# First scale group loaded as two blocks on the ScalarE queue, c moved to the SP queue, statistics of three x tiles moved between engines, engine orders redone

## The chip, the cores and the metric

The kernel runs on one core of one Trainium2 chip. The metric is the device time of one execution in microseconds (us); where several executions are given, the number is their median. Most executions of a kernel agree within a few tenths of a per cent; some runs are called slow (over 1.5% above the fastest of the same kernel) and are left out of ratios. A profile is one execution, and its times count from the start of the span, which is 1.8 to 1.9 us shorter than the device time. Profiles of two kernels therefore show where time lies; the medians and ratios say how much it is.

## The reference, cut to what matters

A diffusion block: c gives modulation vectors, x is normalised, scaled and shifted, then attention and a gated residual follow. B, N, D are 2, 256, 1152, all in bfloat16.

```python
mod = (_silu(c) @ w_mod).reshape(B, 6, 1, D)
shift_a, scale_a, gate_a, shift_m, scale_m, gate_m = [mod[:, i] for i in range(6)]
h = _layernorm(x, axis=-1) * (1 + scale_a) + shift_a
qkv = h @ wqkv
# ... q, k, v cut from qkv
p = _softmax(jnp.einsum('bqd,bkd->bqk', q, k) * D ** (-0.5), axis=-1)
a = jnp.einsum('bqk,bkd->bqd', p, v) @ wo
return x + gate_a * a
```

## The kernel before: the parts that matter

x stands in four tiles of 128 rows (288 KB each). The key projection comes first: the normalised tiles are transposed by TensorE (PE), multiplied by 1 + scale (`s1p`, from `psS`) into `hTs`, and multiplied by the rows of wK (nine loads of 288 KB, one per k). The scale vector is itself a product, of silu(c) and `w_scale`. `w_scale` is loaded in four groups of 128-column blocks; group 0 holds blocks 0 and 1 (576 KB). The first wK steps (k = 0 and 1) need group 0.

```python
nc.scalar.preload_act_table_set("natural_log_exp_and_others")
load_x(syn, 0)                                   # syn: the queue issued by SP
sca.dma_start(out=c_sb, in_=c.rearrange(...))    # sca: the queue issued by ScalarE
# ...
def scale_mods(gi, lo, hi):                      # psS[:, j] += w_scale block j times silu(c)
    k0, k1 = S_GROUPS[gi]                        # ((0, 2), (2, 4), (4, 6), (6, 9))
    for kk in range(lo, hi):
        for j in range(k0, k1):
            ten.matmul(psS[:, j, :], lhsT=wS[gi][:, kk, ...], rhs=sc_rhs(kk), ...)
# ...
junk(2)                      # filler matmuls on a tile of ones, their results are thrown away
ten.transpose(cT_ps, c_sb, ident[...])
# ... three activations make silu(c)
junk(10)
# ... SP's loads, in order: x1, x2, group 0, wK0, wK1, x3, group 1, wK2, group 2, ...
transposes(0, 0)
scale_mods(0, 0, 9)
transposes(0, 1)
k_step(0, 0, P)              # first step with wK
```

Every engine works through its own list in the order in which the program pins it. The scheduler gives each load one of a small set of semaphores, and a load that reuses one waits until the load that used it before has landed.

## Time and profile before

| | kernel before |
|---|---|
| device time, median of the first three runs | 98.47 us (98.41 to 98.59) |
| span of the profile | 95.7 us |
| PE busy | 91.0 us, 95% |
| first matmul on x | 7.69 us |
| scale group 0: issued, landed, used | 2.11, 7.64, 7.91 us |
| scale group 1: landed, used | 11.32, 11.52 us |

First the page. The first lines give the span and the engines' busy time; the rows below cut the span into 40 slices and give tenths of a slice busy. PEclk is the share of the full TensorE clock that was granted. PEld is the load of weights into PE; DVE is VectorE, ACT ScalarE, POOL GpSimd.

```profile
span 95.7 us, 1886 instructions
PE 91.0 (95%) x771; PEld 60.9 (64%) x771; DVE 64.1 (67%) x131; ACT 32.3 (34%) x75; POOL 15.7 (16%) x11
PE   3899999999999999999999999999999999999980
PEclk9999999999999999999999999999999999999999
DMA  1999999999999999999993001122000000303122
```

PE is the limit from end to end, and the loads run flat out for the first half. What counts is when PE's useful work starts and whether it is ever idle after that. The timeline of PE says it (start, duration, engine, operation, output and inputs, shapes; `xN` merges N instructions):

```profile
2.90 0.19 PE L70 MATMUL cT_ps<-ident,c_sb 18*128 18x18 bf16 x1 [0.42 <-DMA c_sb<-in_c_dram]
3.45 4.45 PE L70 MATMUL acc_t<-ones_w 128*128 128x512 bf16 x10
7.69 0.42 PE L70 MATMUL tp_t<-ident,xn 128*128 128x128 bf16 x2
7.91 0.69 PE L70 MATMUL psS<-scT_rep,wS_all 128*128 128x56 bf16 x18
8.44 0.55 PE L70 MATMUL tp_t<-ident,xn 128*128 128x128 bf16 x7
8.98 0.66 PE L70 MATMUL acc_t<-hTs,wK 128*128 128x128 bf16 x9
...
11.52 0.63 PE L70 MATMUL psS<-scT_rep,wS_all 128*128 128x56 bf16 x18
```

Ten fillers end at 7.90, 0.6 us after the first normalised tile is there (7.31); group 0's 18 small matmuls start 0.27 us after its load has landed, and apart from the wait for c in the first line none of these lines shows a wait. The issues of DMA between 2.0 and 2.4 us, with size and time from issue to landing, give the load of group 0 (issued at 2.11, so landed at 7.64) and the one ahead of it, x tile 2, which landed at 5.60:

```profile
wS_all<-in_w_scale_dram SPq DMA_DIRECT2D x1, 576.0 KB, 5.5
x_sb<-in_x_dram SPq DMA_DIRECT2D x1, 288.0 KB, 4.0
```

Last, stretches of 4 us with each engine's busy time, and PEclk third from the end and GB/s last:

```profile
8.00:12.00 4.00, 4.00 (x91) 3.86 (x89) 3.02 (x11) 3.23 (x6) 0.00 (x0) 1.00 1.04 408
12.00:16.00 4.00, 3.93 (x64) 3.55 (x61) 3.56 (x14) 3.26 (x11) 0.00 (x0) 1.00 1.03 402
16.00:20.00 4.00, 4.00 (x60) 3.66 (x58) 1.25 (x9) 1.61 (x5) 0.00 (x0) 1.00 1.04 401
```

PE is busy for nearly all of each stretch at the full clock, while about 400 GB/s come in.

### The profile page before, as it was taken

Reading aid. Unit: us, or ns where it says so; the run is one execution under the profiler, and the core shown is the slowest. Engines: PE = TensorE matmul, PEld = TensorE weight load, DVE = VectorE, ACT = ScalarE, POOL = GpSimd, SP = SyncE. Lnnn points to the kernel's source line nnn. Section 1 sums busy time; section 2 is a strip of 40 time slices with the busy share of each in tenths; the row PEclk is TensorE's granted clock in tenths of the full one; section 3 lists DMA queues with packets and bytes.
Section 4 is the critical chain, followed back from the end, with each engine's and each line's share of the span. In section 5 each row is a group of like instructions: output and inputs, shape, how many; then the busy total and the mean of one; then the engine's idle time right before and its main releaser. Section 6 shows DMA issues by size and latency. Waiting matters only on the chain.

```text
span 95.7 us, 1886 instructions
## 1 busy us (share of the span) xinstructions
PE 91.0 (95%) x771; PEld 60.9 (64%) x771; DVE 64.1 (67%) x131; ACT 32.3 (34%) x75; POOL 15.7 (16%) x11
## 2 busy tenths in 40 slices
PE   3899999999999999999999999999999999999980
PEld 0237989988899644444458765565568766556570
DVE  2487887050552999999999939910009599998780
ACT  5496988020421900003950084342335400000010
POOL 3020000000000000000000000079999900010000
PEclk9999999999999999999999999999999999999999
DMA  1999999999999999999993001122000000303122
GB/s 23 366 337 414 402 397 398 400 420 403 416 416 419 414 413 419 422 422 416 419 400 159 0 0 55 45 65 54 8 0 0 0 0 0 123 7 123 75 100 72
DMA packets 7379, 21.59 MB, mean 225 GB/s; under 512 B 2123, under 2 KB 2891, under 8 KB 7371
## 3 DMA queue, kind: packets, MB, share of 16 engines
q1 hardware_dynamic: 7200, 21.42, 57.7%
q8 instruction: 6, 0.10, 0.4%
q10 hardware_dynamic: 171, 0.05, 0.2%
q14 instruction: 2, 0.02, 0.0%
HBM read 19.76 MB, written 1.44 MB: 221 GB/s over the span
## 4 chain that ended last, share of the span: by engine, by line
PE 93%; DMA 2%; DVE 0%; ACT 0%; issue 0%
PE ps L70 67%; PE acc_t L70 19%; PE psS L70 3%; DMA c_sb<-in_c_dram 2%; PE psH L70 2%; PE tp_t L70 2%; ACT o_sb L70 0%; DVE hTs L70 0%; PE cT_ps L70 0%; DVE s1p L70 0%; ACT L104 0%
## 5 line engine op out<-in xcount | busy, mean ns | idle before, releaser
L70 POOL PARTITION_ALL_REDUCE gate_bc<-gacc x2 | 13.7, 6887 | 56.8 <-DVE gacc L70 56.8
L70 DVE SCALAR_TENSOR_TENSOR gacc<-wg_all,scT_f,gacc 128x1152 f32<-128x1152 bf16 x16 | 22.4, 1416 | 0.4
L70 PE MATMUL ps<-wV,hT 128*128 128x384 bf16 x108 | 17.7, 326 | 0.0
L70 PE MATMUL ps<-hT,wQ 128*128 128x512 bf16 x81 | 17.7, 379 | 0.0
L70 PEld LDWEIGHTS <-wK 128*128 128x128 bf16 x180 | 16.1, 98 | 1.8 <-issue 0.2
L70 PE MATMUL ps<-rows_t,attnT 128*128 128x384 bf16 (+3 forms) x108 | 17.0, 319 | 0.0
L70 PEld LDWEIGHTS <-attnT 128*128 128x128 bf16 x117 | 11.2, 98 | 6.4
L70 PEld LDWEIGHTS <-hT 128*128 128x128 bf16 x108 | 10.6, 98 | 6.9
L70 PE MATMUL acc_t<-hTs,wK 128*128 128x256 bf16 (+1 forms) x144 | 14.8, 259 | 0.1
L70 PEld LDWEIGHTS <-wQ 128*128 128x128 bf16 x81 | 7.9, 98 | 9.4
L70 ACT CAST v_sb<-ps 128x384 bf16<-128x384 f32 x12 | 5.8, 481 | 13.9 <-PE ps L70 13.9
L70 DVE CAST attnT<-ps 128x512 bf16<-128x512 f32 (+1 forms) x6 | 3.5, 603 | 9.5 <-PE ps L70 9.5
L70 ACT CAST qkT<-ps 128x512 bf16<-128x512 f32 x11 | 5.6, 610 | 12.6 <-PE ps L70 12.6
L70 DVE TENSOR_TENSOR ga<-ps,gate_bc 128x384 f32<-128x384 f32 (+3 forms) x12 | 6.4, 537 | 1.1 <-PE ps L70 1.0
L70 PE MATMUL acc_t<-ones_w 128*128 128x512 bf16 x12 | 5.5, 630 | 1.4 <-DVE ones_w L70 1.4
L70 DVE TENSOR_TENSOR o_sb<-ga,x_sb 128x384 bf16<-128x384 f32 (+3 forms) x12 | 6.5, 542 | 0.4
L70 ACT CAST o_sb<-ps 128x192 bf16<-128x192 f32 x1 | 0.3, 319 | 17.3 <-PE ps L70 17.3
L70 DVE CAST qkT<-acc_t 128x512 bf16<-128x512 f32 (+1 forms) x5 | 2.5, 576 | 4.5 <-PE acc_t L70 4.5
L70 DVE BATCH_NORM_STATS2 st_t<-x_sb 128x6 f32<-128x384 bf16 x6 | 3.1, 550 | 2.5 <-DMA x_sb<-in_x_dram 2.5
L70 PE MATMUL ps<-hTs,wK 128*128 128x256 bf16 x36 | 4.3, 272 | 0.0
L70 ACT ACTIVATE hTs<-xnT,s1p 128x128 bf16<-128x128 bf16 (+1 forms) x9 | 3.3, 417 | 2.8 <-DVE s1p L70 2.3
L70 PEld LDWEIGHTS <-ones_w 128*128 128x128 bf16 (+1 forms) x13 | 1.6, 135 | 4.1 <-issue 2.6
(59 smaller groups left out, 76.4 us busy)
## 6 DMA issues: line engine op xcount, KB each, us to landing
wK<-in_wk_dram SPq DMA_DIRECT2D x9, 288.0 KB, 8.3
rows_t<-in_w_shift_dram SPq DMA_DIRECT2D x3, 864.0 KB, 11.7
wQ<-in_wq_dram SPq DMA_DIRECT2D x3, 864.0 KB, 14.3
wg_all<-in_w_gate_dram SPq DMA_DIRECT2D x3, 864.0 KB, 14.4
wV<-in_wv_dram SPq DMA_DIRECT2D x3, 864.0 KB, 17.1
rows_t<-in_wo_dram SPq DMA_DIRECT2D x3, 864.0 KB, 17.1
wS_all<-in_w_scale_dram SPq DMA_DIRECT2D x3, 576.0 KB, 6.4
x_sb<-in_x_dram SPq DMA_DIRECT2D x4, 288.0 KB, 3.6
```

Source lines behind the costliest of these rows:

```text
L70: r = fn(*a, **k)
```

## The change

The intent, as far as the diff tells it: load the two blocks of group 0 from a second queue, so that they come in beside x tile 2 and PE can begin with block 0 alone, one filler earlier; take the statistics of tile 3 off ScalarE (it does tile 2 instead of tiles 1 and 3); redo all engine orders for that. Also c moves from the ScalarE queue to second place on SP.

```diff
+    load_x(syn, 0)
+    syn.dma_start(out=c_sb, in_=c.rearrange("b (k p) -> (b k) p", p=P))
     nc.scalar.preload_act_table_set("natural_log_exp_and_others")
-    load_x(syn, 0)
-    sca.dma_start(out=c_sb, in_=c.rearrange("b (k p) -> (b k) p", p=P))
...
+    def load_block(j):
+        cols = slice(KT * P * j, KT * P * (j + 1))
+        sca.dma_start(out=wS_all[:, cols], in_=w_scale[...])
...
     sca.activation(out=e_sb, in_=cT_ps, func=ACT.Exp, scale=-1.0)
+    load_block(0)
     sca.activation(out=e_sb, in_=e_sb, func=ACT.Ln, bias=1.0)
     sca.activation(out=e_sb, in_=e_sb, func=ACT.Exp, scale=-1.0)
+    load_block(1)
...
-    junk(10)
+    junk(9)
... (the orders; on SP now x2, x1, wK0, wK1, x3, group 1, ...; on PE:)
+    block_mods(0)
+    block_mods(1)
     transposes(0, 0)
+    transposes(0, 1)
... (statistics: tile 1 from ScalarE to VectorE, tile 2 from VectorE to ScalarE,
     tile 3 from ScalarE to VectorE)
```

More of the change, by code (lines that the diff above doesn't have):

```diff
@@ L123 @@
     wS_all = wmpool.tile([P, KT * D], BF16, tag="wS")
-    S_GROUPS = SCALE_GROUPS
+    S_GROUPS = ((0, 2), (2, 4), (4, 6), (6, 9))
     wS = []
@@ L133, in load_scale @@
         syn.dma_start(out=wS_all[:, cols], in_=src)
+    def load_block(j):
+        cols = slice(KT * P * j, KT * P * (j + 1))
+        sca.dma_start(out=wS_all[:, cols], in_=w_scale[P * cols.start : P * cols.stop].rearrange("(p n) -> p n", p=P))
     def load_wK(k):
@@ L277, in scale_mods, with block_mods @@
                 )
+    def block_mods(j):
+        w_j = wS_all[:, KT * P * j : KT * P * (j + 1)].rearrange("p (kk n) -> p kk n", kk=KT)
+        for kk in range(KT):
+            ten.matmul(
+                psS[:, j, :], lhsT=w_j[:, kk, :], rhs=sc_rhs(kk),
+                start=False, stop=(kk == KT - 1), skip_group_check=True,
+            )
     def copy_s1p(gi):
@@ L305, in k_step_b1 @@
             )
-    junk(10)
+    junk(9)
+    load_x(syn, 2)
+    stat_chunk(0, 0)
+    stat_sum(2)
     stat_chunk(0, 1)
-    stat_chunk(0, 0)
     load_x(syn, 1)
-    stat_sum(1)
-    load_x(syn, 2)
     stat_chunk(0, 2)
+    silu_c()
+    block_mods(0)
     stat_aggr(0)
-    silu_c()
-    stat_chunk(2, 2)
-    stat_chunk(2, 1)
     stat_ln(0)
     stat_exp(0)
+    stat_chunk(1, 1)
+    stat_chunk(1, 2)
+    stat_chunk(1, 0)
     norm(0, 0, 2)
+    stat_aggr(1)
+    stat_sq(2)
+    block_mods(1)
     transposes(0, 0)
-    load_scale(0)
-    scale_mods(0, 0, 9)
     norm(0, 2, KT)
-    stat_chunk(2, 0)
-    stat_aggr(2)
+    transposes(0, 1)
     scaled_tp(0, 0, vec)
     scaled_tp(0, 1, vec)
-    stat_sq(1)
-    stat_ln2(1)
+    stat_ln(1)
+    copy_s1p(0)
+    load_wK(0)
     stat_exp(1)
-    copy_s1p(0)
     norm(1, 0, 2)
-    load_wK(0)
-    transposes(0, 1)
-    load_wK(1)
-    norm(1, 2, KT)
-    stat_ln(2)
     k_step(0, 0, P)
     transposes(1, 0)
+    load_wK(1)
+    k_step(1, 0, P)
+    stat_ln2(2)
+    norm(1, 2, KT)
+    stat_exp(2)
+    evac_tp(0, 1, sca, 0, 7)
+    transposes(1, 1)
+    norm(2, 0, 2)
+    evac_tp(1, 1, sca, 0, 7)
+    scaled_tp(1, 1, vec)
     scaled_tp(1, 0, vec)
-    evac_tp(0, 1, sca, 0, 7)
-    k_step(1, 0, P)
     load_x(syn, 3)
-    transposes(1, 1)
+    stat_chunk(3, 2)
+    stat_chunk(3, 0)
+    stat_chunk(3, 1)
+    norm(2, 2, KT)
     k_step(0, P, N)
-    scaled_tp(1, 1, vec)
     k_step(1, P, N)
-    stat_exp(2)
-    norm(2, 0, 2)
-    evac_tp(1, 1, vec, 0, 7)
-    norm(2, 2, KT)
     load_scale(1)
@@ L355 @@
     copy_s1p(1)
-    scaled(2, 0, vec)
     transposes(2, 0)
     transposes(2, 1)
-    evac_tp(2, 1, vec, 0, 7)
-    stat_sum(3)
-    stat_sq(3)
-    stat_ln2(3)
+    stat_aggr(3)
+    stat_ln(3)
     stat_exp(3)
-    norm(3, 0, 2)
+    evac_tp(2, 1, sca, 0, 7)
+    scaled(2, 0, vec)
+    evac_tp(2, 0, vec, 0, 2)
+    scaled_t(0, 2, vec)
     load_wK(2)
     k_step(2, 0, N)
-    norm(3, 2, KT)
-    evac_tp(2, 0, sca, 0, 2)
-    scaled_t(0, 2, vec)
-    transposes(3, 0)
-    load_scale(2)
-    scaled_t(3, 2, vec)
-    scaled(3, 0, sca)
-    evac_tp(3, 0, sca, 0, 2)
-    scaled_t(0, 3, sca)
+    norm(3, 0, 2)
+    scaled(3, 0, sca)
+    load_scale(2)
+    transposes(3, 0)
+    evac_tp(3, 0, sca, 0, 2)
+    norm(3, 2, KT)
     scale_mods(2, 0, 9)
+    transposes(3, 1)
     copy_s1p(2)
+    scaled_t(0, 3, vec)
+    evac_tp(3, 1, vec, 0, 7)
     scaled_t(5, 2, vec)
-    scaled_t(2, 2, sca)
-    transposes(3, 1)
     load_wK(3)
     k_step(3, 0, N)
-    evac_tp(3, 1, vec, 0, 7)
+    scaled_t(1, 2, sca)
+    scaled_t(3, 3, vec)
+    scaled_t(1, 3, sca)
+    scaled_t(3, 2, sca)
     alloc_b1()
     k_step_b1(0, [1, 2, 3, 4])
-    scaled_t(1, 2, vec)
-    scaled_t(3, 3, vec)
-    load_wK(5)
-    scaled(5, 0, vec)
+    scaled(4, 0, sca)
+    scaled_t(5, 3, sca)
+    k_step_b1(3, [1, 2, 3, 4])
     k_step_b1(0, [0])
-    scaled_t(5, 3, sca)
-    k_step(5, 0, N)
-    k_step_b1(3, [1, 2, 3, 4])
-    scaled_t(1, 3, vec)
-    scaled_t(4, 2, sca)
-    scaled_t(2, 3, sca)
+    scaled_t(4, 2, vec)
+    k_step_b1(1, [1, 2, 3, 4])
+    scaled_t(2, 3, vec)
+    k_step_b1(1, [0])
+    load_scale(3)
+    scaled(5, 0, sca)
+    scaled_t(2, 2, vec)
     k_step_b1(2, [1, 2, 3, 4])
-    load_scale(3)
-    k_step_b1(5, [0])
     scale_mods(3, 0, 9)
-    scaled_t(4, 3, vec)
-    scaled(4, 0, sca)
+    scaled_t(4, 3, sca)
     copy_s1p(3)
-    scaled(6, 0, vec)
-    scaled_t(6, 2, vec)
+    scaled(6, 0, sca)
+    scaled_t(6, 2, sca)
     scaled_t(6, 3, vec)
     scaled(7, 0, vec)
-    scaled_t(7, 2, vec)
-    scaled_t(7, 3, vec)
-    scaled(8, 0, vec)
+    scaled_t(7, 2, sca)
+    scaled_t(7, 3, sca)
+    scaled(8, 0, sca)
     scaled_t(8, 2, sca)
-    scaled_t(8, 3, sca)
+    scaled_t(8, 3, vec)
     load_wK(4)
+    load_wK(5)
     load_wK(6)
@@ L417 @@
     load_rest()
-    k_step_b1(1, [0])
-    k_step_b1(1, [1, 2, 3, 4])
     k_step_b1(2, [0])
@@ L424 @@
     k_step_b1(4, [1, 2, 3, 4])
+    k_step(5, 0, N)
+    k_step_b1(5, [0])
     k_step_b1(5, [1, 2, 3, 4])
@@ L669 @@
         pin(rec.seq)
-SCALE_GROUPS = ((0, 2), (2, 4), (4, 6), (6, 9))
+SCALE_BLOCKS = ((0, 1), (1, 2), (2, 4), (4, 6), (6, 9))
 _OUTS = [((2, 256, 1152), 'bfloat16')]
@@ L690, in _packed @@
     scale = rows(w_mod[:, D : 2 * D]).transpose(1, 0, 2)
-    scale = _np.concatenate([scale[:, :, k0 * P : k1 * P].reshape(-1) for k0, k1 in SCALE_GROUPS])
+    scale = _np.concatenate([scale[:, :, k0 * P : k1 * P].reshape(-1) for k0, k1 in SCALE_BLOCKS])
     return {
```

## The prediction

> **What bounds the kernel now.** TensorE. On the page PE is busy 91.0 of 95.7 us; the chain of waits is 93% PE, and from 3.52 us on it has one gap (12.16 to 12.72). Three stages by timeline: filler matmuls until the first data (useful work starts at 7.69; filler starts 0.43 us apart); from 7.7 to 20 us PE rides just behind the loads; then pure matmul to 93 us. The Trainium skill, "TensorE: Matmul & The Clock Gate", Part 1, says cold matmuls run at half rate; the trace agrees (0.43 us per 512 columns before 8.0 us, 0.109 per 256 after). Loads stream at one 288 KB unit per 0.74 us: x0 lands at 3.60, the third unit 5.60, scale group 0 7.64, wK0 8.39, group 1 11.32 (used 11.47), group 3 17.55 (used 18.05). So PE has 0.2 to 0.5 us to gain at most.
>
> **What the change does.**
> 1. One filler of 0.43 us goes.
> 2. c goes behind x0 on one queue. Now it lands at 2.85 alone on its own; behind x0 (last packets start 3.05, landing 3.60) I expect 3.65. The transpose of c and all filler after it start 0.75 later; with one filler less, PE's useful start moves from 7.69 to about 8.05, later.
> 3. The two blocks. Block 0 is issued after the first e_sb activation (4.1), starts about 1.0 us later, shares engines half and half with wK0 and wK1: lands about 7.15. Block 1 reuses the semaphore of x tile 1, which lands third (5.6), so ScalarE stops there until 5.6; it lands about 8.65, against 7.64 for the whole group. The skill, "DMA: Bandwidth & Descriptors", "Issuing engines are not separate DMA queues", says queues interleave on the same engines; bytes are equal, so nothing is gained.
> 4. ScalarE: that stop plus the two issues (0.5 each) and the sum of tile 2 (1.16) come before rstd of tile 0: 7.7 instead of 6.05; norm of tile 0 7.7 instead of 6.56, upper part 8.2 instead of 6.80. First wK step 9.6 instead of 8.98. Its evacuation of tile 0 (0.9) ends about 10.9 and holds the transposes of tile 1.
> 5. VectorE: tile 3 statistics (3 x 0.46 paced) stand at about 11.2 to 12.6, in front of norm of tile 2 and the second s1p copy. The second scale group's matmuls start at 12.3 (11.68 now), the 256-wide step of wK2 at 13.7 (12.72 now).
> 6. Saved: ScalarE's 2.4 us pass over tile 3; not on PE's chain now.
>
> **On the critical path.** Replaying the new order with durations of this trace: PE late by 0.35 at its start, 0.6 at the first wK step, 0.95 at wK2, about 0.8 at wK3 (15.6 instead of 14.83). After that the delay is carried unchanged. 98.47 + 0.8 = 99.3 us.
>
> **Predicted: 99.3 us, range 98.4 to 100.2.** Chances: faster by over 2% 0.01; within 2% 0.94; slower by over 2% 0.05.
>
> **What would show it.** c landing near 3.65 and PE idle from 2.5 to it; first block matmul at 8.05 to 8.2 and a short PE wait before block 1; ScalarE idle before its second issue until x tile 1 lands; first rstd after 7.4; statistics of tile 3 just ahead of the second s1p copy; PE gaps totalling about 1 us between 8 and 14, none after 16.
>
> **What would make it wrong.** c landing before x0, or block 1 by 8.0: then near 98.3. Filler ending before the clock rises, or a gap that delays the rise: useful work at half rate, 1 us or more worse. ScalarE issues far shorter than 0.5 us: 0.3 us better.

## The result

| | before | after |
|---|---|---|
| device time, median of 4 runs each | 98.44 us (98.36 to 98.59) | 105.57 us (105.13 to 106.24) |
| ratio of the fast runs | 1 | 1.0728 (95% interval 1.0661 to 1.0796) |
| span of the profile | 95.7 us | 104.1 us |
| first filler after c, c's transpose | 3.45, 2.90 us | 4.15, 3.59 us |
| first scale matmul | 7.91 us | 11.99 us |
| first wK matmul | 8.98 us | 15.38 us |
| matmuls of scale group 1 start | 11.52 us | 19.69 us |

A ratio is the mean time of one kernel's fast runs over the mean of the other's fast runs of the same rounds, so it is not quite the ratio of the medians. The change makes the kernel 7% slower.

The page after:

```profile
span 104.1 us, 1884 instructions
PE 93.0 (89%) x768; PEld 62.9 (60%) x770; DVE 63.5 (61%) x129; ACT 32.6 (31%) x77; POOL 15.6 (15%) x11
PE   3691169999999999999999999999999999999990
PEclk9999855899999999999999999999999999999999
DMA  3899999999999999999910000112200000203042
```

Two things are new, both in the first eight slices: a hole in the PE row, and a dip of PEclk right behind it. DMA has no hole, so the loads were not missing; others came first. The same two pieces stand in the timeline of PE:

```profile
3.59 0.19 PE L70 MATMUL cT_ps<-ident,c_sb 18*128 18x18 bf16 x1 [1.11 <-DMA c_sb<-in_c_dram]
4.15 4.02 PE L70 MATMUL acc_t<-ones_w 128*128 128x512 bf16 x9
11.99 0.41 PE L70 MATMUL psS<-scT_rep,wS_all 128*128 128x56 bf16 x9 [3.82 <-DMA wS_all<-in_w_scale_dram]
14.03 0.60 PE L70 MATMUL psS<-scT_rep,wS_all 128*128 128x56 bf16 x9 [1.64 <-DMA wS_all<-in_w_scale_dram]
...
15.38 1.17 PE L70 MATMUL acc_t<-hTs,wK 128*128 128x128 bf16 x9
...
19.69 0.63 PE L70 MATMUL psS<-scT_rep,wS_all 128*128 128x56 bf16 x18
```

The fillers end at 8.17, then PE waits 3.82 us for block 0 and 1.64 us for block 1. The nine wK matmuls take 1.17 us, which took 0.66 us before. The stretches of 4 us show why:

```profile
8.00:12.00 4.00, 0.18 (x2) 0.02 (x2) 1.84 (x6) 3.54 (x10) 0.00 (x0) 1.00 1.02 400
12.00:16.00 4.00, 2.36 (x33) 2.25 (x34) 1.12 (x5) 0.37 (x1) 0.00 (x0) 0.54 1.04 415
16.00:20.00 4.00, 4.00 (x54) 4.00 (x52) 2.65 (x8) 1.44 (x2) 0.00 (x0) 0.61 1.04 393
```

PE was idle almost throughout 8 to 12 us; from 12.31 to 19.14 us the clock record is at one half. In that time the useful work, once it could start, ran at half speed.

Why the blocks were late shows in ScalarE's timeline, where lines with ACTq are its DMA issues:

```profile
3.83 0.40 ACTq L70 DMA_DIRECT2D wS_all<-in_w_scale_dram  x1
4.27 0.47 ACT L70 ACTIVATE e_sb<-e_sb 128x18 f32<-128x18 f32 x2 [0.26 <-ACT e_sb L70]
7.50 0.33 ACTq L70 DMA_DIRECT2D wS_all<-in_w_scale_dram  x1
7.89 1.16 ACT L70 ACTIVATE scr<-x_sb 128x1152 f32<-128x1152 bf16 x1 [3.15 <-DMA x_sb<-in_x_dram]
```

Block 0 was issued at 3.83, near the time that I had expected. Block 1 was issued at 7.50, just after x tile 1 had landed at 7.49: it was given that tile's semaphore. What the queues moved between 4.2 and 7.2 us, and the landing time of block 0 (one line of the issues), are the surprise:

```profile
q1 hardware_dynamic: 424, 0.87, 95.4%
...
wS_all<-in_w_scale_dram ACTq DMA_DIRECT2D x1, 288.0 KB, 8.1
```

q1 is SP's queue, q10 ScalarE's. There is no line for q10 at all: for three microseconds after its issue not one packet of block 0 started. Its first packet started at 7.46, and it landed 8.1 us after issue, at 11.94. Block 1 landed at 13.98.

Once block 0 had started, the two queues did run side by side. This is what they moved between 7.5 and 11.5 us:

```profile
q10 hardware_dynamic: 162, 0.34, 24.1%
q1 hardware_dynamic: 408, 1.19, 76.6%
```

The trace's packets, told apart by queue and size and counted off in order, show which loads these were: x tile 3 (issued on SP at 3.43) sent its first packet at 7.25, block 0 (ScalarE, 3.83) at 7.46, group 1 (SP, 3.90) at 7.65. So the load that SP issued 0.07 us after block 0 waited just as long for its start. The last packets of block 0 and of group 1 started at 11.03 and 10.95.

### The profile page after: what moved, and what is told of

Read it like the earlier page. It is cut to its first block, busy times and chain, and to the rows that moved or that the text cites. A ratio compares the mean times of both kernels' runs of the same rounds, so it can differ in the third digit from the quotient of the medians.

```text
span 104.1 us, 1884 instructions
## 1 busy us (share of the span) xinstructions
PE 93.0 (89%) x768; PEld 62.9 (60%) x770; DVE 63.5 (61%) x129; ACT 32.6 (31%) x77; POOL 15.6 (15%) x11
## 4 chain that ended last, share of the span: by engine, by line
PE 83%; DMA 11%; SPq 1%; issue 1%; DVE 0%; ACT 0%
PE ps L70 62%; PE acc_t L70 15%; DMA wS_all<-in_w_scale_dram 6%; DMA x_sb<-in_x_dram 5%; PE tp_t L70 2%; PE psS L70 2%; PE psH L70 2%; SPq L70 1%; ACT o_sb L70 0%; DVE hTs L70 0%; DVE s1p L70 0%; DVE mv_all L70 0%
## 5 line engine op out<-in xcount | busy, mean ns | idle before, releaser
L70 PEld LDWEIGHTS <-wK 128*128 128x128 bf16 x180 | 17.4, 106 | 1.8 <-issue 0.3
L70 PE MATMUL acc_t<-hTs,wK 128*128 128x256 bf16 (+1 forms) x144 | 16.2, 276 | 0.1
L70 PE MATMUL psS<-scT_rep,wS_all 128*128 128x56 bf16 x81 | 3.1, 192 | 5.5 <-DMA wS_all<-in_w_scale_dram 5.5
L70 DVE BATCH_NORM_STATS2 st_t<-x_sb 128x6 f32<-128x384 bf16 x9 | 4.4, 547 | 4.4 <-DMA x_sb<-in_x_dram 4.4
L70 PEld LDWEIGHTS <-wS_all 128*128 128x128 bf16 x81 | 2.7, 99 | 6.5 <-DMA wS_all<-in_w_scale_dram 6.5
L70 ACT ACTIVATE hTs<-xnT,s1p 128x128 bf16<-128x128 bf16 (+1 forms) x14 | 5.0, 430 | 2.0 <-DVE s1p L70 2.0
```

The lines of the kernel that those rows point to most:

```text
L70: r = fn(*a, **k)
```

## The experiments

Each is an edit of the kernel before or of the changed kernel, as its name says, and is compared with runs of the kernel before on the same chip. Landing times are from the trace: time of issue plus time to landing.

The theories: (1) c on the SP queue slows the stream of loads; (2) a load is served in its place in the order of issue, behind the loads issued before it on whichever of the two queues, so late-issued blocks stand at the end of a long line; (3) the ScalarE queue gets only a small share beside a full SP queue. The orders and the statistics are a fourth suspect, and the clock is the fifth.

### after_c_act: only the move of c undone

```diff
-    load_x(syn, 0)
-    syn.dma_start(out=c_sb, ...)
     nc.scalar.preload_act_table_set("natural_log_exp_and_others")
+    load_x(syn, 0)
+    sca.dma_start(out=c_sb, ...)
```

> The changed kernel with one part undone: c goes first on the ScalarE queue again, as in the kernel before. Theory 1 (c behind x0 on the SP queue slows the stream of loads, 250 to 300 GB/s between 2.5 and 7.5 us against 400 before): c lands at 2.85, the third load at about 5.6 instead of 7.49, so ScalarE's second issue is at 5.6 and the blocks land about 1.9 us sooner (10.0 and 12.1); about 103.5 us. Theory 2 (the blocks are late only because a load starts when those issued before it, on whichever queue, have been served): third load and blocks as in the changed kernel, 105 to 105.6 us.

104.56 us, ratio 1.068 (1.057 to 1.079). The third load landed at 6.01 instead of 7.49, block 0 at 11.23 and block 1 at 13.15 (expected 10.0 and 12.1). So c is not the main cause. It may cost a part, 0.5 us by the two ratios and 1.0 by the medians of different rounds, but the intervals of the two ratios overlap, so that part is not shown.

### before_c_sp: only the move of c, in the kernel before

The edit is the reverse of the one above.

> The kernel before with one part of the change alone: c second on the SP queue behind x tile 0, table load after. Theory 1 (c on the SP queue slows the stream): the third load lands near 7.5 instead of 5.60, scale group 0 near 9.5 instead of 7.64, and the time is 100 to 101 us. Theory 2 (only the order of issue matters): c lands 0.75 us later, all else moves by 0.1, time 98.6 to 99.2 us.

98.42 us beside 98.71 for the kernel before on that chip, ratio 1.001 (0.993 to 1.010): no loss that the timing can see. But the stream did slow down: 300 GB/s between 2.5 and 7.5 us instead of 358, the third load landed at 7.08 instead of 5.60, and group 0 at 8.65 instead of 7.64. The profile's span was 1.0 us longer, which the medians do not show (the profile of the kernel before is of a fast execution, see the sum below). Both theories missed here: the landing that I had feared came, the loss of time did not.

### after_blk_sp: only the queue and place of the blocks undone

```diff
     sca.activation(out=e_sb, in_=cT_ps, func=ACT.Exp, scale=-1.0)
-    load_block(0)
...
-    load_block(1)
...
     load_x(syn, 1)
+    load_block(0)          # load_block now issues on syn
+    load_block(1)
```

> The changed kernel with its blocks issued on the SP queue behind x tile 1, ScalarE issuing nothing. If the late blocks are the cause, whatever makes them late: block 0 lands at 8.2 and block 1 at 9.0 instead of 11.94 and 13.98, PE does not go idle for over 1 us, the clock rises once and stays, 99 to 100.5 us. If the redone orders on VectorE and ScalarE are the cause of a good part: above 102 us.

98.72 us beside 98.71, ratio 1.005 (0.996 to 1.014). Blocks landed at 6.98 and 8.64. The 7% hang on the blocks; with them in this place, the new orders, the moved statistics, c and the missing filler together cost nothing that the timing can see.

### after_blk_early: blocks on the ScalarE queue, but issued at once

```diff
+    load_block(0)          # still on sca
+    load_block(1)
     junk(2)
...
     sca.activation(out=e_sb, in_=cT_ps, func=ACT.Exp, scale=-1.0)
-    load_block(0)
...
-    load_block(1)
```

> The changed kernel with its blocks still on the ScalarE queue, but issued at once (about 0.8 and 1.3 us), ahead of most of SP's loads, waiting for nothing. Theory 2 (served in order of issue): they land at 5 to 7 us, x tiles 2 and 1 about 1 us later than now, 98.5 to 100 us. Theory 3 (the ScalarE queue gets a small share of the engines beside a full SP queue): they land after 9 us, 103 us or more.

99.21 us, ratio 1.012 (1.000 to 1.024). Issued at 0.75 and about 1.2 us, the blocks landed at 4.70 and 5.45. Theory 3 falls: between 3.5 and 4.5 us this is what the two queues moved (packets, MB, share of the engines):

```profile
q10 hardware_dynamic: 170, 0.35, 90.4%
q1 hardware_dynamic: 63, 0.05, 15.1%
```

Now the ScalarE queue has nearly everything, while SP's x tile 2, issued at 1.61, is the one that stands behind. Even c, issued at 1.18 after block 0, landed only at about 4.7 and held PE up for 2.2 us, which is probably where this kernel loses its 1%.

### after_pair: both blocks issued together

```diff
     sca.activation(out=e_sb, in_=cT_ps, func=ACT.Exp, scale=-1.0)
     load_block(0)
+    load_block(1)
...
-    load_block(1)
```

> The changed kernel with both blocks issued after the first activation, so that block 1 waits for x tile 2 (lands at 5.0) instead of x tile 1 (7.5) by the semaphore it is given. Theory (loads are served in order of issue): block 0 lands as before (about 11.9), block 1 stands behind scale group 1 and wK2 in place of further loads and lands at about 12.9 instead of 14.0; about 104.5 us. If the wait for the semaphore is not what places block 1: 105.5 us.

104.64 us, ratio 1.064 (1.061 to 1.068). Block 1 was issued at 5.56 instead of 7.50 and landed at 12.47 instead of 13.98; block 0 landed at 10.89. By the medians this is 0.9 us faster. How much of it is the borrowed semaphore's doing is not shown: block 0, issued at 3.83 as in the changed kernel, landed 1.05 us sooner too, and the intervals of the two ratios overlap.

### after_hold and after_hold_x3: block 0 issued as late, a shorter line ahead

To after_pair one tiny ScalarE copy is added behind the two issues. It writes one column of a tile that SP loads next, so SP must hold that load until the blocks have been issued; the load then overwrites the column and the result stays right.

```diff
     load_block(0)
     load_block(1)
+    sca.copy(out=wK[:, 0, 0:1], in_=e_sb[:, 0:1])         # after_hold: SP held before wK0
+    # sca.copy(out=x_sb[:, 3, 0:1], in_=e_sb[:, 0:1])     # after_hold_x3: held before x tile 3
```

> The same as after_pair, but SP is held before wK0 until a tiny ScalarE copy, which follows the two block issues, has written one column of the wK0 tile (the load then overwrites it, the result stays right). So the blocks are issued late as in the changed kernel (about 3.9 and 4.3 us), but only x tiles 2 and 1 stand before them. Theory 2 (served in order of issue): they land right behind x tile 1, at 7 to 9 us, time 98.5 to 100 us. Rival (the ScalarE queue beside a busy SP queue is slow when it is issued late, or the time of issue counts and not what stands ahead): 11 us or later and 103 us or more.

99.59 us, ratio 1.016 (1.007 to 1.024), on the same chip as after_pair with 1.064. Block 0 was issued at about the same time as in the changed kernel and block 1 sooner (it was 7.50 there and 5.56 in after_pair): 3.74 and 4.16 us, as ScalarE's timeline in after_hold shows:

```profile
3.74 0.86 ACTq L70 DMA_DIRECT2D wS_all<-in_w_scale_dram  x2
```

The list of DMA issues of the same profile, cut to the moment of block 0's issue, gives its size and its time to landing:

```profile
wS_all<-in_w_scale_dram ACTq DMA_DIRECT2D x1, 288.0 KB, 4.6
```

The blocks landed at 8.30 and 9.04, not at 11.94 and 13.98. So late issue as such explains no more than the 1.6% that is left; the loads already issued are what counts.

> As after_hold, but SP is held before x tile 3 instead of before wK0, so that two more loads of 288 KB (wK0, wK1) stand before the blocks, which are issued at the same time. Theory 2 (served in order of issue): both blocks land about 1.5 us later than in after_hold, 9.8 and 10.5 us; 99.8 to 101.5 us. Rival (queues share): within 0.5 us of after_hold's 8.30 and 9.04.

102.0 us, ratio 1.035 (1.029 to 1.041). With wK0 and wK1 ahead as well, the blocks, issued at 3.88 and 4.30, landed at 9.72 and 10.78: 1.4 and 1.7 us later than in after_hold, where two loads of 288 KB at the 0.74 us each of the kernel before make 1.5. The time is 0.5 us above the range I gave; PE was idle 1.54 and 0.65 us, and the clock fell for one record of 3.4 us in this kernel too, which I had not counted.

The first packets say the same as the landings. Block 0 sent its first at 4.86 in after_hold, 6.25 in after_hold_x3 and 7.45 in after_pair; the last load issued ahead of it had sent its own first at 4.15 (x tile 1), 6.19 (wK1) and 7.26 (x tile 3).

### before_group_act: the late issue alone, in the kernel before

```diff
     sca.activation(out=e_sb, in_=cT_ps, func=ACT.Exp, scale=-1.0)
+    load_scale(0, sca)     # the whole group 0, one load of 576 KB
...
-    load_scale(0)
```

> The kernel before with one part alone: its first scale group (one load of 576 KB) is issued on the ScalarE queue after the first activation of e_sb (about 3.6 us) instead of fourth on SP. Theory 2 (served in order of issue): x tiles 1 and 2, wK0, wK1, x tile 3 and most of scale group 1 stand before it, it lands at 10 to 11.5 us instead of 7.64, 101 to 103.5 us. Rival (queues share the engines half and half, what I had predicted): it lands near 8.5 us, under 99.5 us.

103.4 us, ratio 1.050 (1.044 to 1.056). Issued at 4.35, the group landed at 11.86 (expected 10 to 11.5); PE waited 4.13 us for it, and the clock fell here too. The loss comes with the old orders, the old place of c and all ten fillers: the issue in that place is enough for 5.0% of the 7.3%.

### after_fill: the wait stays, the clock is kept up

```diff
-    junk(9)
+    junk(25)
...
     stat_sq(2)
+    junk(8)
     block_mods(1)
```

> The changed kernel with 16 more filler matmuls before the first block's and 8 between the first and the second block's, so that PE is not idle while it waits. Theory 1 (of the 7 us, about 2 are useful matmuls at half rate, because PE's idle time lets the clock fall): the blocks land as in the changed kernel (about 11.9 and 14.0), the clock rises once at about 8.9 and stays, the second scale group's matmuls start at 17.3 to 18.0 instead of 19.7, about 103.5 us. Theory 2 (the late landing alone makes the loss): 105.3 us or more.

103.92 us, ratio 1.057 (1.054 to 1.059) against 1.073. The blocks landed as late as ever, 11.45 and 14.05. The timeline of PE in this kernel:

```profile
11.74 1.89 PE L70 MATMUL acc_t<-ones_w 128*128 128x512 bf16 x8
14.10 0.41 PE L70 MATMUL psS<-scT_rep,wS_all 128*128 128x56 bf16 x9 [0.47 <-DMA wS_all<-in_w_scale_dram]
14.34 0.66 PE L70 MATMUL tp_t<-ident,xn 128*128 128x128 bf16 x9
15.00 0.66 PE L70 MATMUL acc_t<-hTs,wK 128*128 128x128 bf16 x9
...
17.58 0.63 PE L70 MATMUL psS<-scT_rep,wS_all 128*128 128x56 bf16 x18
```

Its stretches of 4 us, with PEclk third from the end:

```profile
12.00:16.00 4.00, 3.53 (x44) 2.30 (x43) 1.35 (x6) 0.91 (x1) 0.00 (x0) 1.00 1.04 419
16.00:20.00 4.00, 3.94 (x71) 3.63 (x69) 3.94 (x14) 2.29 (x5) 0.00 (x0) 1.00 1.06 396
```

Useless matmuls make the kernel 1.6 us faster (1.073 to 1.057 of 98.4 us, in different rounds), since the nine wK matmuls take 0.66 us again and group 1 starts at 17.58 instead of 19.69. By this, about a quarter of the loss is the clock; the rest goes with the late landing.

### after_orders, once more in five rounds, and orders_norm_first

after_orders is after_blk_sp with c back on the ScalarE queue: what is left of the change is the orders, the statistics and one filler less.

> The changed kernel with both load changes undone: c first on the ScalarE queue, blocks on SP behind x tile 1. What is left is the redone orders, the moved statistics and one filler less. If the orders are worth something: under 98.0 us. If, as I predicted, VectorE's statistics of tile 3 and ScalarE's order delay PE: 99 us. Equal to before within 0.5 us: the orders are neutral.

97.93 us, ratio 0.995 (0.992 to 0.999), the best kernel so far. It was repeated (after_orders_5). In the same rounds ran a variant of it (orders_norm_first) with one small change of VectorE's order:

```diff
-    stat_chunk(1, 1)       # and (1, 2), (1, 0): statistics of tile 1 before the first norm
     norm(0, 0, 2)
...
     norm(0, 2, KT)
+    stat_chunk(1, 1)       # now behind both norms of tile 0
```

> The kernel of after_orders once more, on another chip and in five rounds, because its ratio of 0.995 is small: a real gain shows again as 0.992 to 0.998, chance as 1.000 or more.

> after_orders with VectorE's statistics of x tile 1 moved behind both norms of tile 0, since in after_orders the norm waited for them (7.74 instead of a ratio ready at 6.04) and PE was idle 0.22 us. If that idle time counts: 0.2 us faster than after_orders of the same rounds. If the landing of scale group 1 (11.50, used at 11.59) is the limit: equal within 0.15 us.

The repeat gave 97.88 us and a ratio of 0.999 (0.994 to 1.004); the variant 98.30 us and 1.002 (0.998 to 1.006). So the gain of half a per cent was not confirmed, and no version shown here beats the kernel before. That would fit a pace set by the loads. The chain of after_orders, which follows the last instruction back to what released it, begins with the issues and one load and reaches group 1's matmuls at 11.75:

```profile
1.64 4.68 DMA x_sb<-in_x_dram
...
11.75 0.48 PE psS L70 x18
```

Group 1 landed at 11.50 in that profile and its matmuls started at 11.59 in the timeline, as against 11.32 and 11.52 before: one filler less changed nothing there.

### bcs_16rows and bcs_first: why c slows the stream

Of the fourteen profiles so far (the kernel before, the changed one and twelve experiments), eight have c on SP; seven of these moved 261 to 300 GB/s between 2.5 and 7.5 us, and all six with c on the ScalarE queue 325 to 387. The odd one was after_blk_early with 380. Two single profiles tried two explanations, with edits of before_c_sp:

```diff
     load_x(syn, 0)
-    syn.dma_start(out=c_sb, ...)
+    syn.dma_start(out=c_sb[0:16], in_=c_rows[0:16])     # bcs_16rows
...
+    sca.dma_start(out=c_sb[16:], in_=c_rows[16:])
```

In bcs_first, c stands before `load_x(syn, 0)` instead of behind it.

> The kernel before with c second on SP as in before_c_sp, but 16 of its 18 rows there and the last two on the ScalarE queue[...]. Theory A (the 18-row load engages only some of the engines and leaves the stream behind it uneven): 325 GB/s or more between 2.5 and 7.5 us, the third x tile lands by 6.2. Theory B (any small load in that place does it): 300 GB/s or less, third x tile near 7.

> The kernel before with c first on SP, x tile 0 behind it. Theory C (it matters that c stands between two large loads): 325 GB/s or more between 2.5 and 7.5 us. Theory A (the 18 rows on some of the engines make it uneven wherever it stands): 300 GB/s or less.

300 GB/s and 277 GB/s; the third x tile landed at 6.19 and 6.38. Neither explanation holds for the rate. Why the stream is slower with c on SP stays open; so does whether it is c itself or the empty ScalarE queue. With one profile each, this is a look and no measurement of time (98.69 and 99.83 us in single runs of unknown state; in bcs_first the clock fell for 3.41 us as well).

## Why the prediction was wrong

The time was forecast as 99.3 us (98.4 to 100.2); it is 105.57.

- **"starts about 1.0 us later, shares engines half and half with wK0 and wK1: lands about 7.15 ... it lands about 8.65" (step 3) is the step that failed**, and in it the start. Block 0's first packet came 3.63 us after its issue; it landed at 11.94 and block 1 at 13.98. From what the skill says of interleaving queues I had made an equal share from 1.0 us after the issue on. The runs show that loads start in the order of issue over both queues: around the late blocks, no load's first packet came more than 0.4 us ahead of that of a load issued before it. So there was no packet of block 0 from 4.2 to 7.2 us; 90% of the engines' time for the same queue when it was issued first (after_blk_early); landing at 8.30 with two large loads unfinished ahead and 9.72 with four (after_hold, after_hold_x3); and a loss of 5.0% in the kernel before from that one issue (before_group_act). The sharing did come, but from 7.46 on and with x tile 3 and group 1, and stretched block 0's packets over 3.6 us, where a load of 288 KB in the stream of the kernel before took 0.74. By what mechanism the order of issue carries over from one queue to the other, no run shows.
- **x tile 1 at 5.60** was mis-sized: I took the landing of the third load from the profile of before, where c was not on SP. It was 7.49, and with c moved back 6.01. By the reuse of its semaphore this also put off the issue of block 1, from the 5.6 that I had to 7.50; what that cost in time stays open (after_pair was 0.9 us faster, with overlapping intervals). That ScalarE would stop there was right, and it stood still longer than I said.
- **The clock.** "a gap that delays the rise: useful work at half rate, 1 us or more worse" was listed as a risk and not counted. It came in another form: the clock had risen, at 8.90, and fell again. Once the blocks land at 12 and 14 us it follows: PE was idle 3.82 us, the record is at one half from 12.31 to 19.14, and keeping PE busy gained 1.6 us. The Trainium skill, "TensorE: Matmul & The Clock Gate", Part 1, states an idle window of about 3.4 us; the idle time and the lengths of the records (3.41 us and twice that) agree with it, but shorter waits did it too (3.08 us in after_pair; see the last section).
- **The sum, from the two profiles.** Matmuls of block 1 start at 14.03 where group 0's started at 7.91: 6.12 us. From there to group 1's matmuls it is 5.66 us instead of 3.61: 2.05 us, nearly all of it at half clock. Together 8.17 us, and the span grew by 8.4. The medians differ by 7.1 us; the profiled execution of before was faster than any of the four timed ones (97.58 us against 98.36 and more).
- **Right:** c at 3.65 (transposed at 3.59) and the fillers' end near 8.05 (8.17); that one filler less gains nothing; that the pass over tile 3 that ScalarE is spared was not on PE's chain; that the delay is carried unchanged once PE streams. ScalarE's issues took 0.40 and 0.33 us instead of 0.5.
- **Overcharged:** steps 4 and 5 charged the orders with most of 0.8 us. With the loads in place (after_orders) the wK2 step started at 12.86 instead of 12.72. The statistics of tile 3 do stand ahead of the second part of tile 2's norm, and in after_blk_early and after_fill the chain does pass through them (1.39 us); in after_orders it runs instead through those of tile 1 (1.00 us), which orders_norm_first moved without gain.

## What to carry to other kernels

In these runs a second DMA queue was no overtaking lane: before moving a load to it, list the loads that will have been issued by then on all queues and add up their time, and put what is needed first at the head of the order of issue. Look at which semaphore a load waits for as well, because a shared one can tie it to a load it has nothing to do with. Where PE waits for data, count the clock too: here a wait of 3.8 us was followed by 6.8 us at half clock, and filler matmuls bought 1.6 us of the loss back.

## What the Trainium skill lacked or had wrong

- "DMA: Bandwidth & Descriptors", "Queues, rings and completion order" says that each DMA engine round-robins between the queue rows it has work for, packet by packet. No run here contradicts that: once block 0's packets had started, the queues did mix (24% and 77% of the engines' time from 7.5 to 11.5 us). What I found on no page is when a load issued on one queue counts as work while the other is full. Here a 288 KB load issued at 3.83 us started its first packet at 7.46, in its place in the order of issue, and landed 8.1 us after issue with five large loads unfinished ahead; it landed 4.6 us after issue with two ahead, 5.8 with four.
- "DMA: Bandwidth & Descriptors", "Issuing engines are not separate DMA queues" says that loads from several engines interleave on the same engines. The bytes per time agree (about 400 GB/s with one or two queues in use), but it lacks the warning that the order of issue over the queues still sets the order of starts (to within 0.4 us here).
- No page found tells of the slower stream with a 4.5 KB load on the SP queue: 261 to 300 GB/s between 2.5 and 7.5 us in nine of ten profiles, against 325 to 387 with that load on the ScalarE queue. The cause is open.
- "TensorE: Matmul & The Clock Gate", Part 1, agrees with the changed kernel: the granted clock rose at 8.90 us, fell at 12.31 after a wait of 3.82 us and stayed at half for 6.83. A whole idle window of about 3.4 us is not needed, though: in after_hold_x3 the clock fell, for 3.41 us, after waits of only 1.54 and 0.65 us that lay close together, and in bcs_first after waits of 1.24 and 0.87. Part 1 also tells of a kernel in which micro-idles between groups of matmuls were enough; it lacks how long they were.
